# Attention outputs stored later, a third buffer for the final rows, and q and v laid out in pairs of blocks

## The chip, the cores and the metric

The kernel is one launch on one core of a Trainium2 chip. The metric is device time of the whole launch in microseconds, lower is better.

## The reference

Three stages follow one another on 2304 tokens (4 sequences of 576) of width 512, all in float32:

```
attn_out = windowed attention, 8 heads of 64 (4 with the last 32 tokens,
           4 with every 4th of the last 128), softmax, times v
x   = attn_out as (2304, 512)
e   = argmax(x @ w_gate)                      # one of 8 experts for each token
x   = softmax gate * sigmoid gate * (relu(x @ w1[e]) @ w2[e])    # 512 -> 1024 -> 512
out = relu(x @ w_in) ** 2 @ w_out             # 512 -> 2048 -> 512
```

## The kernel before

**Attention** (`attention`, L307) goes through 18 blocks of 128 tokens. Iteration i of its loop (L632, i = 0 to 14) does, in PE's order: `tr(i)` (L449, four transposes of block i's probabilities), the scores of block i + 2 (`qk`, L416), the transposes of block i - 1's output (`xt`, L503), and probabilities times v (`pv_mm`, L465). DVE, POOL and ACT make the softmax between them. Every few blocks a group of tokens is routed: router scores (`lg`, L518), ranks (`route4`, L569 to L572), and `scatter` (L611), an indirect DMA from POOL that writes each token's number into its expert's list in `meta_d`. Blocks 15 to 17 follow the loop in code written out by hand (from L676).

**Transfers** go nearly all through SP's queue, which issues in program order. Each DMA signals one of eight semaphores in turn, so it is issued only when the one eight places ahead of it has landed. The loads are q (`load_q`, L328), k (`load_k`, L335) and v with a column of ones (`load_v`, L346), usually two blocks at a time; v goes to every second partition, so a load of it is two DMAs. A buffer's next load waits until PE has read the last: q has three buffers of two blocks, `vb` holds four blocks, `kz` six. A **store** of a block pair (`store`, L491) writes the attention output `x` to `x_d` in HBM with three DMAs: 256 KB for the heads of the plain window (L495, 128 rows outermost), and for each block 128 KB for the dilated heads (L497), whose outermost dimension is 4, the rows inside it 32. Before, `x` has three buffers of two blocks, and the pair of blocks i - 2 and i - 1 is stored in iteration i = 2, 4, ..., 14.

**The way into the experts.** `choose` (L176) picks the fullest expert from the counts without the last three blocks. SP then reads its number and loads its first weights (`raw`, L117), its list (`mt`, L137) and more weights. POOL gathers 240 token rows from `x_d` (`gather(0)`, L143, two indirect DMAs), which may name any token of blocks 0 to 14 and so waits for all their stores. ACT and DVE split the weights (`conv_w`, L124 and L125) and the transposed tokens into two parts, and the first expert matmul starts (L792). From there PE runs nearly without a gap through the experts and the two passes of the last layer.

**The last layer's second pass** (`down2`, L898) adds, for each of six token blocks of 384, three final tiles of 128 rows: DVE adds the first pass's part into `os` (L919), and POOL scatters `os` to `out` (L920). `os` has two buffers (tag `ys`). `narrow` (L285) uses tag `fa`, also two buffers, only until the first pass ends.

Of the kernel before, what the change touches and what calls it, by code (L numbers as in the profile page):

```python
# [10 lines left out]
F32 = mybir.dt.float32  # L11
F32R = mybir.dt.float32r
# [10 lines left out]
B, H, S, D = 4, 8, 576, 64  # L23
P = 128
NT = B * S
NB = NT // P
# [4 lines left out]
COLS = [{1: 1, 2: 2}.get(len(r), 4) for r in GROUPS]  # L31
NG = len(GROUPS)
EARLY = GROUPS[NG - 1][0]
E = 8
DM = H * D
FF = 1024
# [9 lines left out]
NSPILL = 32  # L46
TB = 384
NTB = NT // TB

FA = 6  # L50

# [2 lines left out]
def attention_experts_kernel(ctx: ExitStack, tc: tile.TileContext, qB, kB, vB, wg, wE, wF, consts, rows, ids, out):  # L54
    nc = tc.nc
    cpool = ctx.enter_context(tc.tile_pool(name="cpool", bufs=1))
    dpool = ctx.enter_context(tc.tile_pool(name="dpool", bufs=1, space=DRAM))
    rp = ctx.enter_context(tc.tile_pool(name="rp", bufs=1))
# [25 lines left out]
    nspill = cpool.tile([1, 1], I32, name="nspill")  # L84
    mt = cpool.tile([P, E + 1, 3, 4], I32, name="mt")

    slots = [rp.tile([P, 2, 1024], F32R, name=f"slot{i}") for i in range(8)]
    free = list(range(8))

    def raw_tile():  # L90
        return stg.tile([P, 1024], F32, tag="raw", name="raw", bufs=3)
# [215 lines left out]
    def attention():  # L307
        st = ExitStack()
        c2 = st.enter_context(tc.tile_pool(name="c2", bufs=1))
# [4 lines left out]
        masks = c2.tile([P, 4, 2, 64], F32, name="masks")  # L314
        tri32 = c2.tile([P, P], F32, name="tri32")
        kz = c2.tile([P, 2, 4, (LAP + 1) * P], F32, name="kz")
        vb = c2.tile([P, 4, 2, 4, 4, D + 1], F32, name="vb")
        q_t = {}

        def warm(n):  # L320
# [4 lines left out]

        def load_q(i, n):
            q = wk.tile([P, 2, 4, P], F32, tag="q", name="q", bufs=3)
            nc.sync.dma_start(out=q[:, 0:n].rearrange("p i a s -> p i (a s)"), in_=qB[i:i + n].rearrange("i p s -> p i s"))  # L328
            for j in range(n):
                q_t[i + j] = q[:, j]  # L330

# [11 lines left out]
        def load_v(i, n, engine=nc.sync):  # L343
            j = i % 4
            for h2 in range(2):
                engine.dma_start(  # L346
                    out=vb[h2:P:2, j:j + n, h2].rearrange("p i a c e -> p i (a c e)"),
                    in_=vB[i:i + n, h2].rearrange("i m e -> m i e"),
                )

        def clear_k(t, first, second):
# [1 line left out]
            second.memset(kz[:, 1, :, P * t:P * t + P], 0.0)  # L353

        def clear_v(j, h2, engine):
            engine.memset(vb[:, j, h2], 0.0)

        load_q(0, 1)
        clear_k(1, nc.vector, nc.gpsimd)
# [94 lines left out]
        def pv_mm(i, apart=False):  # L454

            pt = pt_t.pop(i)
            if apart:
                o = [ps_s.tile([P, 2, 256], F32, tag="s", name="o2") for _ in range(2)]
            else:
                t = ps_1.tile([P, 4, 256], F32, tag="o", name="o")  # L460
                o = [t[:, 0:2], t[:, 2:4]]
            v = vb[:, i % 4]
            for p in range(4):
                for c in range(4):
                    nc.tensor.matmul(  # L465
                        out=o[p // 2][32 * c:32 * c + 32, p % 2, 0:130], lhsT=pt[:, p, 32 * c:32 * c + 32], rhs=v[:, :, p, c, :], start=True, stop=True
                    )
            o_t[i] = [t] if not apart else o

        def pv_x(i):  # L470
            for a, o in enumerate(o_t.pop(i)):
                n = o.shape[1]
                oh = o[:, :, 0:130].rearrange("p a (h e) -> p a h e", h=2)
                rs = wk.tile([P, 4, 2, 1], F32, tag="rs", name="rs")[:, 0:n]
                nc.vector.tensor_scalar(out=rs, in0=oh[:, :, :, 64:65], scalar1=1e-9, scalar2=None, op0=ALU.add)
                rr = wk.tile([P, 4, 2, 1], F32, tag="rr", name="rr")[:, 0:n]
                nc.vector.reciprocal(out=rr, in_=rs)
                if i % 2 == 0 and a == 0:
                    x_t["pair", i // 2] = wk.tile([P, 2, DM], F32, tag="x", name="x", bufs=3)
                x = x_t["pair", i // 2][:, i % 2]  # L480
                nc.vector.tensor_tensor(
                    out=x[:, 256 * a:256 * a + 128 * n].rearrange("p (a h d) -> p a h d", a=n, h=2), in0=oh[:, :, :, 0:64],
                    in1=rr.to_broadcast([P, n, 2, 64]), op=ALU.mult,
                )
            x_t[i] = x
# [5 lines left out]
        def store(i, m, engine=nc.sync):  # L491
            a = i % 2
            x = x_t["pair", i // 2]
            d = x_d[P * i:P * i + m * P]
            engine.dma_start(out=d[:, 0:256].rearrange("(n p) c -> p n c", n=m), in_=x[:, a:a + m, 0:256])  # L495
            for n in range(m):
                engine.dma_start(out=d[P * n:P * n + P, 256:512].rearrange("(j r) c -> r j c", r=4), in_=x[:, a + n, 256:512])  # L497
# [134 lines left out]
        for i in range(EARLY):  # L632
            tr(i)
            ex(i + 1)
            qk(i + 2)
            t = (i + 2) % LAP
            n = i + 2 - t + LAP
            if t == 2 and n < NB:
                load_k(n, 2)
            if t == 4 and n + 2 < NB:  # L640
                wrap()
                load_k(n + 2, min(3, NB - n - 2))
            if i > 0 and i % 2 == 0:
                store(i - 2, 2)
            if i % 2 == 0 and i + 6 < NB:
                load_q(i + 6, 2)
            if i == 0:
                load_consts()
            if i == 3:
                clear()  # L650
            if i == 3:
                nc.vector.tensor_copy(tri, tri32)
                nc.vector.tensor_copy(cs[:, 0, :], io8)
            for a, g in ((2, ends.get(i - 2)), (4, ends.get(i - 3))):
                if g is not None and g < NG - 3:
                    scatter(g, range(a - 2, min(a, COLS[g])))
            if i > 0:
                xt(i - 1)
            g = ends.get(i - 1)
            if g is not None:  # L660
                route4(g)
            pv(i)
            if i % 2 == 1 and i + 3 < NB:
                load_v(i + 3, 2)
            if i in ends:
                lg(ends[i])
                route1(ends[i])
                route2(ends[i])
                route3(ends[i])
            if g is not None:  # L670
                route5(g)
                route6(g)
                if g == NG - 3:
                    scatter(g)
# [68 lines left out]
    def experts():  # L743
# [2 lines left out]
        rp2 = st.enter_context(tc.tile_pool(name="rp2", bufs=1, reuse_waits="tile"))  # L746
        wp = st.enter_context(tc.tile_pool(name="wp", bufs=1, reuse_waits="tile"))
        ps = st.enter_context(tc.tile_pool(name="ps", bufs=1, space=PSUM, reuse_waits="tile"))
        for i in range(8, 16):
            slots.append(rp2.tile([P, 2, 1024], F32R, name=f"slot{i}"))  # L750
            free.append(i)

# [145 lines left out]
        def down2(b, f, js=range(TB // P)):  # L898
# [3 lines left out]
            for j in js:  # L902
# [4 lines left out]
                nc.tensor.matmul(out=o_t[j], lhsT=h[:, a], rhs=w[:, 1], start=False, stop=False)  # L907
                nc.tensor.matmul(out=o_t[j], lhsT=l[:, a], rhs=w[:, 0], start=False, stop=last)  # L908
                if last:
                    s = wp.tile([P, 512], F32, tag="ys", name="os", bufs=2)  # L910
                    t = b * (TB // P) + j
                    if f < FA:
                        if j % 2:
# [200 lines left out]
def _layout(inputs):  # L1114
# [17 lines left out]

    q, k, v = heads["q"], heads["k"], heads["v"]
    qb = np.concatenate([pairs(plain(q, 0, P), P), pairs(dilated(q, 0, 32).reshape(NB, H // 2, P, D), P)], axis=3)
    qB = np.ascontiguousarray(qb).reshape(NB, P, 4 * P)
    kp = k[:H // 2].reshape(2, 2, NT, D).transpose(1, 3, 0, 2)
    kd = dilated(k, 0, 32).reshape(NB, 2, 2, P, D).transpose(2, 4, 1, 0, 3).reshape(2, D, 2, NT)
    kB = np.ascontiguousarray(np.concatenate([kp, kd], axis=2))
# [1 line left out]
    vp = plain(one, -32, 160)  # L1140
    vp = np.stack([vp[:, :, 32 * c:32 * c + 64] for c in range(4)], axis=2)
    vb = np.concatenate([vp, dilated(one, -32, 64)], axis=1)
    vB = np.ascontiguousarray(vb.reshape(NB, 4, 2, 4, 64, D + 1).transpose(0, 2, 4, 1, 3, 5)).reshape(NB, 2, 64, 16 * (D + 1))
    g = np.zeros((DM, 32), f)
    g[:, 0:E] = inputs["moe_w_gate"]
    g[:, E:2 * E] = inputs["moe_w_output_gate"]
# [48 lines left out]
```

## Time and profile before

| what | us |
|---|---|
| three runs | 778.11, 779.4, 782.96 |
| median | 779.4 |
| the profiled execution | 777.51 |
| its span (first to last instruction) | 775.8 |
| attention's loop, from its first `tr` to the one after it | 13.0 to 82.6 |
| first expert matmul | 113.6 |
| PE's last matmul | 762.9 |

In the rows below, a timeline row gives start and duration in us, engine, line, operation, tiles, shapes and count, and in brackets the idle time before it with what ended it. SPq rows are DMAs being issued, not moved. A window row gives the stretch, its length, then busy us (and instructions) of PE, PEld (weight loads), DVE, ACT and POOL, the clock granted to PE as a share, the mean busy share of the 16 DMA engines, and GB/s. A row of waits gives who waited for whom, us in total, times, and the longest.

### The profile page before, as it was taken

What the parts mean: (1) busy time and instruction counts of PE and PEld (TensorE: products, weight loads), DVE (VectorE), ACT (ScalarE), POOL (GpSimd) and SP (SyncE); (2) the same over time, 40 slices, a digit from 0 to 9 for tenths busy, and PEclk for the clock granted to TensorE, in tenths of its full rate; (3) what the DMA queues carried; (4) which work ended last, traced back from release to release, by engine and by line L of the source; (5) the groups of instructions that cost most, each with busy time, mean ns of one, the idle gap of its engine ahead of it and who ended that gap; (6) DMA issues with size and microseconds to landing.
All of it is one profiled execution on the core that took longest, in us unless ns stands there. A gap on an engine that the chain in (4) does not pass through costs nothing. (4 is left out here: it accounts for less than half of the span.)

```text
span 775.8 us, 13876 instructions
## 1 busy us (share of the span) xinstructions
PE 725.0 (93%) x5371; PEld 658.2 (85%) x5371; DVE 435.3 (56%) x888; ACT 327.2 (42%) x647; POOL 95.5 (12%) x104
## 2 busy tenths in 40 slices
PE   7877659999999999999999999999999999999993
PEld 4655539999999999999989998999899998888892
DVE  6756747776657666867686768732424233333321
ACT  2533425554455565655555555632223223223220
POOL 5233535011011010000000000000101010000101
PEclk9999979999999999999999999999999999999997
DMA  8999567575565676775344443230303020120201
GB/s 273 289 284 263 141 195 217 171 248 189 162 223 177 210 240 202 208 229 149 116 125 146 154 135 117 74 123 1 122 1 123 1 95 28 47 77 0 83 1 44
DMA packets 55057, 110.15 MB, mean 142 GB/s; under 512 B 9513, under 2 KB 30890, under 8 KB 54986
## 3 DMA queue, kind: packets, MB, share of 16 engines
q1 hardware_dynamic: 45338, 93.35, 39.2%
q0 software_dynamic: 4176, 10.57, 3.9%
q10 hardware_dynamic: 5472, 5.29, 2.0%
q8 instruction: 44, 0.72, 0.4%
q14 instruction: 27, 0.22, 0.1%
HBM read 89.42 MB, written 19.80 MB: 141 GB/s over the span
## 5 line engine op out<-in xcount | busy, mean ns | idle before, releaser
L792 PE MATMUL hp<-xh,slot 128*128 128x384 f32 (+6 forms) x672 | 214.2, 319 | 2.9 <-DVE hl L807 1.6
L794 PE MATMUL hp<-xh,slot 128*128 128x384 f32 (+6 forms) x672 | 213.9, 318 | 0.0
L793 PE MATMUL hp<-xl,slot 128*128 128x384 f32 (+6 forms) x672 | 213.3, 317 | 0.0
L792 PEld LDWEIGHTS hp<-xh,slot 128*128 128x128 f32 x672 | 126.6, 188 | 6.9 <-DVE hl L807 2.0
L793 PEld LDWEIGHTS hp<-xl,slot 128*128 128x128 f32 x672 | 126.5, 188 | 3.0
L794 PEld LDWEIGHTS hp<-xh,slot 128*128 128x128 f32 x672 | 126.4, 188 | 0.0
L879 DVE SCALAR_TENSOR_TENSOR g<-hp,r 128x384 f32<-128x384 f32 x96 | 53.3, 555 | 119.9 <-ACT r L878 119.4
L906 PE MATMUL op<-slot,gh 128*128 128x512 f32 x288 | 112.5, 391 | 2.3 <-ACT gh L881 2.3
L908 PE MATMUL op<-slot,gl 128*128 128x512 f32 x288 | 114.0, 396 | 0.0
L907 PE MATMUL op<-slot,gh 128*128 128x512 f32 x288 | 113.4, 394 | 0.0
L125 DVE TENSOR_TENSOR slot<-raw,slot 128x1024 fp32r<-128x1024 f32 x64 | 77.8, 1225 | 52.5 <-ACT slot L124 52.2
L878 ACT ACTIVATE r<-hp 128x384 f32<-128x384 f32 x96 | 46.9, 489 | 141.8 <-PE hp L794 141.1
L793 PE MATMUL yp<-hl,slot 128*128 128x240 f32 (+6 forms) x288 | 85.1, 295 | 2.3 <-DVE hl L807 2.3
L792 PE MATMUL yp<-hh,slot 128*128 128x240 f32 (+6 forms) x288 | 86.1, 299 | 0.1
L794 PE MATMUL yp<-hh,slot 128*128 128x240 f32 (+6 forms) x288 | 84.7, 294 | 0.0
L883 DVE TENSOR_TENSOR gl<-g,gh 128x384 fp32r<-128x384 f32 x96 | 53.5, 558 | 44.0 <-ACT gh L881 43.5
L881 ACT CAST gh<-g 128x384 fp32r<-128x384 f32 x96 | 49.2, 513 | 63.3 <-DVE g L879 62.9
L920 POOL DMA_INDIRECT out<-os,idc x18 | 17.6, 977 | 467.9 <-DVE os L919 466.4
L124 ACT CAST slot<-raw 128x1024 fp32r<-128x1024 f32 x64 | 66.4, 1050 | 16.3 <-DMA raw<-in_wE 12.1
L906 PEld LDWEIGHTS op<-slot,gh 128*128 128x128 f32 x288 | 54.2, 188 | 12.6 <-ACT gh L881 3.5
L908 PEld LDWEIGHTS op<-slot,gl 128*128 128x128 f32 x288 | 54.0, 188 | 12.5 <-DVE gl L883 1.2
L907 PEld LDWEIGHTS op<-slot,gh 128*128 128x128 f32 x288 | 54.0, 188 | 9.6
(152 smaller groups left out, 875.0 us busy)
## 6 DMA issues: line engine op xcount, KB each, us to landing
raw<-in_wE SPq DMA_DIRECT2D x63, 512.0 KB
raw<-in_wF SPq DMA_DIRECT2D x32, 512.0 KB
yr<-yT_d SPq DMA_DIRECT2D x48, 192.0 KB
vb<-in_vB SPq DMA_DIRECT2D x16, 520.0 KB
part_d<-os SPq DMA_DIRECT2D x18, 256.0 KB
raw<-part_d SPq DMA_DIRECT2D x18, 256.0 KB
q<-in_qB SPq DMA_DIRECT2D x8, 512.0 KB
x_d<-x SPq DMA_DIRECT2D x22, 128.0 KB
```

The lines of the kernel that those rows point to most:

```text
L124: nc.scalar.copy(out=hi, in_=raw)
L125: nc.vector.tensor_tensor(out=lo, in0=raw, in1=hi.bitcast(F32), op=ALU.subtract)
L792: nc.tensor.matmul(out=out, lhsT=wh, rhs=mh, start=first, stop=False)
L793: nc.tensor.matmul(out=out, lhsT=wh, rhs=ml, start=False, stop=False)
L794: nc.tensor.matmul(out=out, lhsT=wl, rhs=mh, start=False, stop=last)
L878: nc.scalar.activation(out=r, in_=p[:, :TB], func=ACTF.Relu)
L879: nc.vector.scalar_tensor_tensor(out=q, in0=p[:, :TB], scalar=0.0, in1=r, op0=ALU.max, op1=ALU.mult)
L881: nc.scalar.copy(out=h, in_=q)
L883: nc.vector.tensor_tensor(out=l, in0=q, in1=h.bitcast(F32), op=ALU.subtract)
L906: nc.tensor.matmul(out=o_t[j], lhsT=h[:, a], rhs=w[:, 0], start=first, stop=False)
L907: nc.tensor.matmul(out=o_t[j], lhsT=h[:, a], rhs=w[:, 1], start=False, stop=False)
L908: nc.tensor.matmul(out=o_t[j], lhsT=l[:, a], rhs=w[:, 0], start=False, stop=last)
```

## The change

The stores of blocks 0 to 13 move from iterations 2 to 14 to iterations 9 to 14, by a table; `x` gets nine buffers of two blocks instead of three, and the room comes from weight slots: only three of the sixteen exist during attention, the rest are made after it. q and v are laid out in HBM (and v on the chip) so that two blocks of one partition stand in one run of bytes: a pair of q is 128 rows of 4 KB instead of 256 of 2 KB, a half of a pair of v 64 rows of 8320 bytes instead of 128 of 4160. The third final tile of each token block takes tag `fa` in place of `ys`.

```diff
+STORES = {9: (0,), 10: (2,), 11: (4,), 12: (6,), 13: (8, 10), 14: (12,)}
+VN = 16 * (D + 1)
+VL = -(-2 * VN // 128) * 128
...
-    slots = [rp.tile([P, 2, 1024], F32R, name=f"slot{i}") for i in range(8)]
-    free = list(range(8))
+    slots = [rp.tile([P, 2, 1024], F32R, name=f"slot{i}") for i in range(3)]
+    free = list(range(3))
...
-        vb = c2.tile([P, 4, 2, 4, 4, D + 1], F32, name="vb")
+        vb = c2.tile([P, 2, 4, 4, 4, D + 1], F32, name="vb")
...
-            nc.sync.dma_start(out=q[:, 0:n].rearrange("p i a s -> p i (a s)"), in_=qB[i:i + n].rearrange("i p s -> p i s"))
+            a = i % 2
+            nc.sync.dma_start(out=q[:, 0:n].rearrange("p i a s -> p (i a s)"), in_=qB[i // 2, :, a:a + n].rearrange("p i s -> p (i s)"))
...
-                    out=vb[h2:P:2, j:j + n, h2].rearrange("p i a c e -> p i (a c e)"),
-                    in_=vB[i:i + n, h2].rearrange("i m e -> m i e"),
+                    out=vb[h2:P:2, h2, j:j + n].rearrange("p i a c e -> p (i a c e)"),
+                    in_=vB[i // 2, h2, :, VN * (i % 2):VN * (i % 2 + n)],
...
-                    x_t["pair", i // 2] = wk.tile([P, 2, DM], F32, tag="x", name="x", bufs=3)
+                    x_t["pair", i // 2] = wk.tile([P, 2, DM], F32, tag="x", name="x", bufs=NB // 2)
...
-            if i > 0 and i % 2 == 0:
-                store(i - 2, 2)
+            for a in STORES.get(i, ()):
+                store(a, 2)
...
-        for i in range(8, 16):
+        for i in range(3, 16):
             slots.append(rp2.tile([P, 2, 1024], F32R, name=f"slot{i}"))
...
-                    s = wp.tile([P, 512], F32, tag="ys", name="os", bufs=2)
+                    s = wp.tile([P, 512], F32, tag="fa" if j == 2 and f >= FA else "ys", name="os", bufs=2)
```

`clear_v`, `pv_mm` and the host's layout of q and v follow the new order of dimensions.

SP's queue before, from the load of v for blocks 6 and 7 on (`vb` is v, `kz` k, `x_d<-x` a store, `zm` the zeros of the lists):

```order
L346 DMA vb<-in_vB 64x2x1040 x2
L495 DMA x_d<-x 128x2x256
L497 DMA x_d<-x 4x32x256 x2
L328 DMA q<-in_qB 128x2x512
L335 DMA kz<-in_kB 64x4x256 x2
L346 DMA vb<-in_vB 64x2x1040 x2
L495 DMA x_d<-x 128x2x256
L497 DMA x_d<-x 4x32x256 x2
L328 DMA q<-in_qB 128x2x512
L335 DMA kz<-in_kB 64x4x384 x2
```

The same place after the change (line numbers are those of the changed kernel):

```order
L352 DMA vb<-in_vB 64x2080 x2
L334 DMA q<-in_qB 128x1024
L341 DMA kz<-in_kB 64x4x256 x2
L352 DMA vb<-in_vB 64x2080 x2
L334 DMA q<-in_qB 128x1024
L341 DMA kz<-in_kB 64x4x384 x2
```

Each round of loads loses the store that stood in it, and q and v have half as many, longer rows.

SP's queue before, from the last load of k to the first weights:

```order
L335 DMA kz<-in_kB 64x4x128 x2
L495 DMA x_d<-x 128x2x256
L497 DMA x_d<-x 4x32x256 x2
L346 DMA vb<-in_vB 64x2x1040 x2
L495 DMA x_d<-x 128x2x256
L497 DMA x_d<-x 4x32x256 x2
L495 DMA x_d<-x 128x256
L497 DMA x_d<-x 4x32x256
L94 TENSOR_LOAD e_t
L117 ISA
L117 DMA raw<-in_wE 128x1024
```

The same place after:

```order
L341 DMA kz<-in_kB 64x4x128 x2
L501 DMA x_d<-x 128x2x256
L503 DMA x_d<-x 4x32x256 x2
L501 DMA x_d<-x 128x2x256
L503 DMA x_d<-x 4x32x256 x2
L501 DMA x_d<-x 128x2x256
L503 DMA x_d<-x 4x32x256 x2
L352 DMA vb<-in_vB 64x2080 x2
L501 DMA x_d<-x 128x2x256
L503 DMA x_d<-x 4x32x256 x2
L501 DMA x_d<-x 128x256
L503 DMA x_d<-x 4x32x256
```

Three stored pairs now stand between the last k and the last v, where one stood, and three more pairs stand ahead of that k; the reading of the expert's number and its weights still come behind the store of block 14. The order of instructions on PE, DVE, ACT and POOL is the same in both kernels.

## Rows read from the trace of the kernel before

**Rows 1.** Windows: the loop's first iterations, then the rest of it

```profile
13.00:26.00 13.00, 13.00 (x264) 10.23 (x268) 8.53 (x17) 6.88 (x15) 4.81 (x8) 0.87 0.96 322
26.00:86.00 60.00, 44.94 (x1014) 35.16 (x1006) 38.55 (x135) 24.12 (x62) 24.07 (x24) 0.97 0.91 274
```

**Rows 2.** Timeline: `tr` of iterations 0, 2 and 3, and of block 15

```profile
13.00 0.80 PE L449 MATMUL pt<-ident,pr 128*128 128x128 f32 x4 [2.33 <-DMA ident<-in_consts]
...
20.28 0.66 PE L449 MATMUL pt<-ident,pr 128*128 128x128 f32 x4
...
23.49 0.66 PE L449 MATMUL pt<-ident,pr 128*128 128x128 f32 x4
...
82.61 0.66 PE L449 MATMUL pt<-ident,pr 128*128 128x128 f32 x4
```

**Rows 3.** Waits of PE from 13 to 87 us, those that DMAs ended

```profile
PE o L465 <- DMA vb<-in_vB: 5.6, 3, 2.0
PE s L416 <- DMA kz<-in_kB: 2.6, 3, 1.5
...
PE s L416 <- DMA q<-in_qB: 2.2, 2, 1.5
```

**Rows 4.** DMA view of 10 to 22 us, loads alone; GB/s in 40 slices

```profile
GB/s 372 395 391 406 359 287 353 410 383 369 373 407 413 442 395 405 363 408 376 396 404 385 325 353 360 395 374 291 378 367 356 375 347 383 363 379 375 410 379 372
DMA packets 2538, 4.52 MB, mean 377 GB/s; under 512 B 215, under 2 KB 1423, under 8 KB 2537
```

**Rows 5.** DMA view of 30 to 86 us: total, and the stores issued

```profile
DMA packets 9836, 15.21 MB, mean 272 GB/s; under 512 B 978, under 2 KB 7017, under 8 KB 9825
...
x_d<-x SPq DMA_DIRECT2D x14, 128.0 KB
x_d<-x SPq DMA_DIRECT2D x6, 256.0 KB
```

**Rows 6.** Windows at the end of the loop's transfers

```profile
88.00:90.00 2.00, 1.31 (x37) 0.94 (x35) 1.97 (x8) 0.96 (x3) 1.79 (x2) 1.00 0.31 87
90.00:92.00 2.00, 1.07 (x8) 0.83 (x8) 1.82 (x11) 1.07 (x2) 0.99 (x1) 1.00 0.23 75
92.00:93.00 1.00, 1.00 (x35) 0.82 (x33) 0.86 (x8) 0.65 (x2) 0.92 (x1) 1.00 0.07 12
```

**Rows 7.** Timeline from the last store of the loop to the first expert matmul

```profile
85.02 0.50 SPq L497 DMA_DIRECT2D x_d<-x  x1
...
88.80 1.09 PE L465 MATMUL o<-vb,pts 128*32 128x130 f32 x32 [0.58 <-ACT pts L451]
...
93.37 0.38 SPq L117 DMA_DIRECT2D raw<-in_wE  x1
...
95.95 0.39 SPq L137 DMA_DIRECT2D mt<-meta_d  x1
...
100.10 1.04 ACT L124 CAST slot<-raw 128x1024 fp32r<-128x1024 f32 x1 [3.21 <-DMA raw<-in_wE]
...
101.95 1.37 POOL L143 DMA_INDIRECT xg<-x_d,mt  x1 [8.90 <-DMA x_d<-x]
...
113.61 0.38 PE L792 MATMUL hp<-xh,slot 128*128 128x240 f32 x1 [1.35 <-DVE xl L159]
```

**Rows 8.** Waits from 395 to 776 us, the two around `os`

```profile
DVE os L919 <- DMA out<-os,idc: 25.8, 6, 5.4
...
PE op L906 <- ACT gh L881: 2.3, 3, 0.9
```

**Rows 9.** Timeline: one of PE's three gaps in the second pass

```profile
684.50 0.50 PE L906 MATMUL op<-slot,gh 128*128 128x512 f32 x1 [0.94 <-ACT gh L881]
```

**Rows 10.** Timeline of the last three tiles

```profile
762.46 0.39 PE L908 MATMUL op<-slot,gl 128*128 128x512 f32 x1
762.50 0.97 POOL L920 DMA_INDIRECT out<-os,idc  x1 [0.39 <-DVE os L919]
764.03 0.69 DVE L919 TENSOR_TENSOR os<-op,raw 128x512 f32<-128x512 f32 x1 [1.81 <-DMA out<-os,idc]
765.00 0.97 POOL L920 DMA_INDIRECT out<-os,idc  x1 [1.53 <-DVE os L919]
```

More of the change, by code (lines that the diff above doesn't have):

```diff
@@ L355, in clear_v @@
         def clear_v(j, h2, engine):
-            engine.memset(vb[:, j, h2], 0.0)
+            engine.memset(vb[:, h2, j], 0.0)
         load_q(0, 1)
@@ L461, in pv_mm @@
                 o = [t[:, 0:2], t[:, 2:4]]
-            v = vb[:, i % 4]
+            v = vb[:, :, i % 4]
             for p in range(4):
@@ L1134, in _layout @@
     qb = np.concatenate([pairs(plain(q, 0, P), P), pairs(dilated(q, 0, 32).reshape(NB, H // 2, P, D), P)], axis=3)
-    qB = np.ascontiguousarray(qb).reshape(NB, P, 4 * P)
+    qB = np.ascontiguousarray(qb.reshape(NB // 2, 2, P, 4 * P).transpose(0, 2, 1, 3))
     kp = k[:H // 2].reshape(2, 2, NT, D).transpose(1, 3, 0, 2)
@@ L1142, in _layout @@
     vb = np.concatenate([vp, dilated(one, -32, 64)], axis=1)
-    vB = np.ascontiguousarray(vb.reshape(NB, 4, 2, 4, 64, D + 1).transpose(0, 2, 4, 1, 3, 5)).reshape(NB, 2, 64, 16 * (D + 1))
+    vB = np.zeros((NB // 2, 2, 64, VL), f)
+    vB[..., :2 * VN] = vb.reshape(NB // 2, 2, 4, 2, 4, 64, D + 1).transpose(0, 3, 5, 1, 2, 4, 6).reshape(NB // 2, 2, 64, 2 * VN)
     g = np.zeros((DM, 32), f)
```

## Prediction

> **What bounds the kernel now.** I read the windows first, then the waits, the DMA view and the timeline at the place where attention hands over to the experts, and last the waits of the second pass of the last layer.
>
> The windows split the loop in two [rows 1]. From 13 to 26 us PE is busy throughout and 322 GB/s arrive. From 26 to 86 us PE is busy 44.94 of 60 us, so it idles 15.1 us, while the DMA engines are busy 91% of the time; yet they move less, 274 GB/s. The timeline gives the pace: iteration 2, still without a wait, lasts 23.49 - 20.28 = 3.21 us, and the 13 iterations up to `tr` of block 15 last 62.3 us, or 4.79 each [rows 2]. Of the idle 15.1 us the waits put 5.6 + 2.6 + 2.2 = 10.4 us down to loads of v, k and q [rows 3]. So the loop is bound by its transfers, and could end 10.4 to 15.1 us earlier.
>
> Why do the busy engines move less? With loads alone they move 377 GB/s [rows 4]. From 30 to 86 us they move 15.21 MB at 272 GB/s [rows 5]; at 377 that would take 40.3 us instead of 56, so 15.7 us are lost. The stores there are 14 x 131 KB + 6 x 262 KB = 3.41 MB, 9.0 us at 377. By this a stored pair (6.5 of them in that stretch) costs (15.7 + 9.0) / 6.5 = 3.8 us of all engines, instead of 1.4. The windows at the end, when nearly only stores are left, show what a store is: 31% and then 23% of the engines busy, 4 or 5 of 16, at 87 and 75 GB/s [rows 6]. The dilated half, with an outermost dimension of 4, uses about four engines; a load issued behind it is complete only when its share on those four is through.
>
> The way into the experts is the second bound [rows 7]. The last store of the loop is issued at 85.02, and the windows show engines at work until about 92.5 [rows 6]. The first weights are issued at 93.37, and ACT gets them at 100.10 after a wait of 3.21; the list is issued at 95.95, and the gather starts at 101.95 after 8.90 us of idle POOL. The view names the store for that wait, but stores have long been done by 92.5: what came last can only be the list. The first expert matmul comes at 113.61, 11.66 us behind the gather, and from there PE hardly stops. A microsecond at the gather is a microsecond of the kernel.
>
> **The change part by part.**
>
> *Stores out of the loop's first half.* Nothing is computed differently, and PE, DVE, ACT and POOL keep their order; SP's queue loses one stored pair (3 DMAs) from each round of loads up to iteration 8, and gets three more pairs between the last k and the last v. Until iteration 9 the loads should run as in [rows 4], and the loop's waits of [rows 3] go: I take the loop to end about 10 us earlier, at 72 to 73.
>
> That is no gain yet, since the gather needs every store of blocks 0 to 14. What those stores ask of the four engines is the same bytes, in the same pieces, and so the same work. In the loop of before these four were the busy ones nearly throughout (loads lasted as long as they did), and nothing in the change takes work from them. They have the same total to do from 13 us on, so I take the last store to land where it did, at about 92.5, though PE is done far earlier. What does move is the issue of weights and list. Before, they were issued at 93.37 and 95.95, when nearly nothing was left to move; now the fullest expert is known about 10 us earlier, and both stand in the queue behind the last stores (at most eight DMAs are under way, so they are issued when the train has about eight left). They land when their bytes have followed the stores: two blocks of 524 KB of weights, 2 x 1.4 us at 377 GB/s, make 92.5 + 2.8 = 95.3. The gather starts at 95.3 instead of 101.95: **-6.6 us**. Ends for this term: 0, if the list still takes 6 us behind the last store, and -15.1, the whole idle time of the loop, if the four engines had time to spare.
>
> The Trainium skill ("DMA: Bandwidth & Descriptors", section "Why a DMA increments its semaphore by 16 and not by 1") says that a DMA is spread over the largest number of engines up to 16 that divides the slowest dimension of both its sides, and on the lowest-numbered ones. For the dilated store that is 4, and always the same 4; the 23% busy share [rows 6] agrees. It speaks against this change: putting such stores later makes none of them wider, and a train of them queues on the four engines. If the engines were instead shared evenly, the sum would be that of the second rival below.
>
> *v of blocks 16 and 17* stands behind six pairs. By the same reckoning (the four engines' work ahead of it is unchanged) it lands about where it did, and `pv_mm(16)`, at 88.80 before [rows 7], stays near there while PE waits some 10 us in front of it. Behind it on PE are only blocks 16 and 17 and their routing, which the gather does not need. Cost 0; the third rival is the price if this is wrong.
>
> *Paired rows.* q and v go in rows of twice the length: in the stretch of [rows 5], 7017 of 9836 packets are under 2 KB, and it is not shown what longer ones cost. The slices of loads alone reach from 287 to 442 GB/s [rows 4]; on the 14.3 MB of q and v of the whole attention, against 377, that is from 11.9 us longer to 5.5 us shorter. But these are the loads, which PE no longer waits for in either case if the stores are gone from beside them: I take 0, the mean of the row, and keep the ends for the range.
>
> *Nine x buffers and fewer weight slots.* DVE's writes of `x` wait for no store any more, and the three slots that exist are all that the attention stage fills; the others are made after it, where a first write may wait for a late store of the same room. DVE's writing of `x` was not among the waits that mattered: 0.
>
> *The third final buffer.* In the second pass DVE waits 25.8 us in six places for a scatter to leave `os`; PE feels it only in three gaps of 2.3 us together, the longest 0.9 [rows 8], one of them at 684.50 [rows 9]. With the third buffer DVE writes all three tiles of a token block at once: **-2.3 us** (from 0, if ACT's `gh` is late for a reason of its own, to -2.3). At the very end DVE waits 1.81 us and starts the last tile at 764.03, 1.2 us behind PE's last matmul, which starts at 762.46 and takes 0.39; it would then start at 762.95 and end at 763.64. POOL's scatter before it ends at 763.47, so the last one starts at about 763.64 + 0.28 (its distance from DVE's end before) = 763.9 instead of 765.00 [rows 10]: **-1.1 us**. In all -3.4 us. The use of tag `fa` ends with the first pass, so it takes no buffer from anybody.
>
> *Sum.* -6.6 - 2.3 - 1.1 = -10.0 us. The profiled execution took 777.51 (span 775.8 and 1.7 around it), which becomes 767.5. The median of the three runs stands 1.9 above the profiled one; I carry that over: 779.4 - 10.0 = **769.4 us**.
>
> **The rivals.**
>
> *Everything that the loop gains reaches the gather.* For it: the waits [rows 3] are loads, and 272 against 377 GB/s [rows 4, 5] may be a matter of switching between reads and writes, which a train of writes alone avoids. Against it: the train alone runs at 75 to 87 GB/s [rows 6]. The gain at the head is then 10.4 to 15.1, say 12.8, and with the tail 16.2: 763.2 us.
>
> *The head gains nothing.* The four engines get further behind than I think, or the list stays 6 us behind the last store as it was (93.37 and 95.95 may not be set by the loop at all). For it: 6 us from issue to use with little traffic, after 92 us only 12 GB/s [rows 6, 7]. Only the tail's 3.4 us are left: 776.0 us.
>
> *Slower: v of blocks 16 and 17 waits behind the train.* Iteration 9 begins between 20.28 + 7 x 3.21 = 42.8 and 20.28 + 7 x 4.79 = 53.8, say at 48. From there to that load stand six pairs and the loads of about two pairs of blocks (q 0.52, k 0.52, v 1.07 MB each pair, 4.2 MB, 11 us at 377). If a pair costs not 3.8 us but all its 524 KB at 75 GB/s, 7.0 us [rows 6], v lands at 48 + 6 x 7.0 + 11 = 101, and `pv_mm(16)` starts 12.2 us late. ACT's wait of 3.21 us for weights [rows 7] is the slack I can see; 9.0 us remain and reach the first expert matmul, less 3.4 of the tail: 785.0 us. It decides from about 6 us for a pair: then v lands at 95, and 3 us of loss cancel the tail's gain. Against it: 3.8 us is what pairs cost in the loop, and the load of v overlaps the train on the other twelve engines.
>
> **How the numbers follow.** About 1% (7.8 us: 771.6 and 787.2) is what a measurement of this kernel can tell from no change. Forecast 0.50, full gain 0.18, only the tail 0.22, slower by v 0.10. The forecast's own range is 765 to 775, so some 0.7 of it counts as faster; with the full gain that is 0.35 + 0.18, and 0.53 in all. Same: 0.15 of the forecast, 0.22 of the tail alone and a little of the v case, 0.39. Slower by more than 1% needs v later than about 103, by longer packets' bad end [rows 4] or a dearer pair: 0.08. The range reaches from just below the full gain, 761, to 782, between the tail alone and the v case.
>
> **What would show it.** Right: no waits of PE for v, k or q in the loop and `tr` of block 15 near 72; stores issued from iteration 9 on and a stretch of 10 us or more with about a quarter of the engines busy; a long wait of PE at `pv_mm(16)`, and the last store near 92; weights and list issued well before 93, the gather near 95, the first expert matmul near 107; in the second pass no wait of DVE for `out`, and the last scatter about 1.1 us closer to PE's last matmul. Wrong: a gather at or behind 101.95 (head gains nothing), or near 88 (the four engines were not full); a first expert matmul that waits for `pv_mm(16)`; waits for loads that remain in iterations 3 to 8, where no store runs, which would mean that the loads themselves are the limit.

## The result, and the profile after

The changed kernel takes 773.72 us (median of 6) beside 781.57 for the kernel before: a ratio of 0.9892, 95% interval 0.9861 to 0.9922, or 8.4 us less (the two medians are 7.9 apart). Measured once more beside other kernels (experiment e9) it took 775.0 beside 779.0: 0.9949, interval 0.9926 to 0.9971, 4.0 us less. The two intervals just miss each other: the gain is clear of noise, but its size is known only as 4.0 in one measurement and 8.4 in the other (2.3 to 10.9 by their intervals). The forecast was 10.0 less, with a range of 761 to 782.

The profiled execution took 771.45 us, its span is 769.8. First the windows, which answer to [rows 1]:

```profile
13.00:26.00 13.00, 12.74 (x301) 10.03 (x302) 9.63 (x19) 7.21 (x16) 5.52 (x9) 1.00 0.92 325
26.00:86.00 60.00, 49.41 (x1032) 36.00 (x1024) 39.62 (x141) 23.66 (x61) 25.64 (x26) 0.98 0.85 259
```

PE is busy 49.41 of 60 us instead of 44.94, so the loop did become freer. The timeline has the transposes of block 15 at 76.47 instead of 82.61 [rows 2]:

```profile
76.47 0.66 PE L455 MATMUL pt<-ident,pr 128*128 128x128 f32 x4
```

The waits of PE from 13 to 87 us (compare [rows 3]) show what went and what came:

```profile
PE o L471 <- issue: 4.2, 9, 1.0
PE s L422 <- DMA kz<-in_kB: 1.5, 1, 1.5
PE lg L524 <- issue: 1.4, 4, 0.4
PE pt L455 <- issue: 1.2, 1, 1.2
...
PE o L471 <- DMA vb<-in_vB: 0.3, 1, 0.3
```

Waits for loads fell from 10.4 to 1.8 us. But 6.8 us now end on "issue", which is idle time for which the profile shows no cause; before it was 2.8. Both are one execution: in e9 the same program has 5.8 for loads and 5.0 on "issue". The last part of the way to the experts answers to [rows 6, 7], first as windows, then as a timeline:

```profile
84.00:86.00 2.00, 1.65 (x15) 1.24 (x15) 1.34 (x7) 0.21 (x1) 0.00 (x0) 0.50 0.87 144
86.00:88.00 2.00, 0.60 (x7) 0.45 (x5) 1.97 (x10) 1.10 (x3) 1.04 (x1) 0.50 0.84 294
88.00:90.00 2.00, 0.00 (x0) 0.00 (x0) 1.82 (x10) 0.24 (x1) 1.17 (x2) 0.50 0.42 152
90.00:92.00 2.00, 0.14 (x4) 0.17 (x8) 0.31 (x3) 0.00 (x0) 0.80 (x1) 0.50 0.37 121
```

```profile
89.83 0.97 POOL L617 DMA_INDIRECT meta_d<-idsb,di  x1 [0.30 <-issue]
91.12 0.54 SPq L122 DMA_DIRECT2D raw<-in_wE  x1
91.86 1.96 PE L471 MATMUL o<-vb,pts 128*32 128x130 f32 x32 [5.26 <-DMA vb<-in_vB]
95.97 0.39 SPq L142 DMA_DIRECT2D mt<-meta_d  x1
100.37 1.05 POOL L148 DMA_INDIRECT xg<-x_d,mt  x1 [9.57 <-DMA x_d<-x]
112.16 0.38 PE L799 MATMUL hp<-xh,slot 128*128 128x240 f32 x1 [1.35 <-DVE xl L164]
```

The list is issued at 95.97, where it was issued before at 95.95. The gather starts only 1.58 us earlier and the first expert matmul 1.45 us. PE waits 5.26 us for v of blocks 16 and 17, and its granted clock is half from 84 to beyond 92.

At the other end the waits of DVE for `out` [rows 8] and PE's gaps [rows 9] are gone, and the last tiles (compare [rows 10]) follow one another:

```profile
757.03 0.69 DVE L927 TENSOR_TENSOR os<-op,raw 128x512 f32<-128x512 f32 x1 [0.67 <-PE op L915]
757.99 0.97 POOL L928 DMA_INDIRECT out<-os,idc  x1 [0.38 <-DVE os L927]
```

So of the profiled execution's 6.06 us, 1.45 were gained at the head and the rest behind it. And 1.45 is not more than two executions of the same attention code differ by: in e3, whose attention is that of the kernel before, the first expert matmul comes at 115.37 instead of 113.61, and in e9, the changed kernel again, at 114.37, which is later than before.

### The profile page after: what moved, and what is told of

The parts are those of the page before. It is cut to its first block, busy times and chain, and to the rows that moved or that the text cites. A ratio compares the mean times of both kernels' runs of the same rounds, so it can differ in the third digit from the quotient of the medians.

```text
span 769.8 us, 13866 instructions
## 1 busy us (share of the span) xinstructions
PE 726.6 (94%) x5371; PEld 659.5 (86%) x5371; DVE 437.4 (57%) x888; ACT 327.6 (43%) x647; POOL 95.3 (12%) x104
## 4 chain that ended last, share of the span: by engine, by line
PE 81%; DMA 6%; DVE 5%; issue 2%; ACT 2%; another core or an unknown queue 1%; SPq 1%; ACTq 0%; POOL 0%; POOLq 0%; DVEq 0%
PE hp L799 12%; PE hp L801 12%; PE hp L800 12%; PE op L914 9%; PE op L915 9%; PE op L913 9%; PE yp L800 4%; PE yp L799 4%; PE yp L801 4%; PE o L471 1%; PE xp L172 1%; PE s L422 1%; DVE slot L130 1%; DMA q<-in_qB 1%; DMA raw<-in_wE 1%
## 5 line engine op out<-in xcount | busy, mean ns | idle before, releaser
L913 PE MATMUL op<-slot,gh 128*128 128x512 f32 x288 | 112.0, 389 | 0.0
L130 DVE TENSOR_TENSOR slot<-raw,slot 128x1024 fp32r<-128x1024 f32 x64 | 77.8, 1225 | 47.9 <-ACT slot L129 47.2
L129 ACT CAST slot<-raw 128x1024 fp32r<-128x1024 f32 x64 | 66.4, 1051 | 12.5 <-DMA raw<-in_wE 8.8
L915 PEld LDWEIGHTS op<-slot,gl 128*128 128x128 f32 x288 | 54.0, 188 | 11.4
```

The costliest lines, as they stand in the source:

```text
L129: nc.scalar.copy(out=hi, in_=raw)
L130: nc.vector.tensor_tensor(out=lo, in0=raw, in1=hi.bitcast(F32), op=ALU.subtract)
L913: nc.tensor.matmul(out=o_t[j], lhsT=h[:, a], rhs=w[:, 0], start=first, stop=False)
```

## The experiments

Each ratio is to the kernel before, run beside the experiment.

**e1 and e2: the dilated stores made wider.** Four DMAs a pair, 32 rows outermost, instead of two with 4:

```diff
-            for n in range(m):
-                engine.dma_start(out=d[P * n:P * n + P, 256:512].rearrange("(j r) c -> r j c", r=4), in_=x[:, a + n, 256:512])
+            for r in range(4):
+                engine.dma_start(out=d[:, 256:512].rearrange("(n j r) c -> r j n c", n=m, r=4)[r], in_=x[32 * r:32 * r + 32, a:a + m, 256:512])
```

> The changed kernel, with the dilated half of each stored pair written by four DMAs of 32 rows outermost (64 KB each, one per residue of the token number by 4) in place of two with 4 outermost; same bytes, same places in the queue. If the four engines are what the train of stores costs (theory A), the stretch of a quarter-busy engines at 80 to 98 us goes: v of blocks 16 and 17 lands before 86 (91.7 now), the last store before 92 (97.8 now), PE's wait of 5.3 us for v and most of its 4.2 us without instructions go, the first expert matmul comes at 104 to 108 instead of 112.2, and the kernel takes 765 to 770 us. If the head is held by something else, the list's scatter and load or the pace of PE alone (theory B), the first expert matmul stays within 1.5 us of 112.2 and the time at 772 to 775.

> The kernel before, with only that same edit of the dilated stores: they stay in iterations 2 to 14. Theory A: the 15.7 us that stores cost the loop beyond their bytes go, PE's waits for v, k and q in the loop fall from 10.4 to under 3 us, the block 15 transposes start near 73 to 76 instead of 82.6, the first expert matmul at 104 to 107 instead of 113.6, and the kernel takes 771 to 774 us against 781.6. Theory B: waits as before, first expert matmul within 1.5 us of 113.6, time within 0.5% of before.

Measured: e1 772.22, ratio 0.9878 (0.984 to 0.9916), the changed kernel's own; first expert matmul at 113.65, and PE waits for v 10.8 us in all. e2 779.98, ratio 0.9993 (0.9974 to 1.0012): no change. Windows of e2 at the end of the loop's transfers, to be held against [rows 6]:

```profile
84.00:86.00 2.00, 1.41 (x44) 0.86 (x42) 1.38 (x8) 1.68 (x5) 1.39 (x3) 1.00 0.35 100
86.00:88.00 2.00, 1.09 (x11) 0.47 (x11) 0.00 (x0) 0.00 (x0) 1.70 (x2) 1.00 0.20 44
88.00:90.00 2.00, 1.01 (x14) 0.74 (x12) 0.72 (x4) 0.13 (x1) 0.23 (x1) 0.72 0.04 4
90.00:92.00 2.00, 1.36 (x14) 1.12 (x16) 1.93 (x9) 0.78 (x3) 0.79 (x1) 0.50 0.00 0
```

The stores were through by 90, some 2.5 us sooner than before, though SP was done issuing them at 86.3 instead of 85.5. The Trainium skill's rule on the number of engines ("DMA: Bandwidth & Descriptors", section "Why a DMA increments its semaphore by 16 and not by 1") agrees with that, but no gain follows from it. With the transfers at 0 to 4 GB/s from 88 to 92, the gather of e2 still came later than before:

```profile
93.23 0.99 POOL L613 DMA_INDIRECT meta_d<-idsb,di  x1 [0.98 <-DVE rs L475]
94.52 0.97 POOL L613 DMA_INDIRECT meta_d<-idsb,di  x1 [0.30 <-issue]
104.03 1.05 POOL L143 DMA_INDIRECT xg<-x_d,mt  x1 [8.53 <-DMA x_d<-x]
```

From the last scatter of blocks 13 and 14 to the gather it is 9.5 us with idle transfers; it was 9.9 in the kernel before and 10.5 after the change. In e5 and e11 below, which have no stores in the loop, it is 9.5 and 10.6. That is a chain of latencies (scatter, list, gather), and no train of stores is needed for it. In its form of four engines, theory A falls.

**e3: the third final buffer alone.**

```diff
-                    s = wp.tile([P, 512], F32, tag="ys", name="os", bufs=2)
+                    s = wp.tile([P, 512], F32, tag="fa" if j == 2 and f >= FA else "ys", name="os", bufs=2)
```

> The kernel before, with only the third final buffer (every third final tile of the second pass under the other tag). By the prediction: DVE's waits for out go, PE's three gaps of 2.3 us in the second pass go, and the last scatter starts 1.1 us closer to PE's last matmul: 3.4 us less, ratio near 0.9956. Rival: the gaps go, but the end of the program stays 13 us behind PE's last matmul as it did in the changed kernel, so only 2.3 us: ratio near 0.997.

Measured: 776.34, ratio 0.9943 (0.9922 to 0.9965): 4.4 us less, 2.7 to 6.1. The buffer alone gives half of the gain first measured, and all of the second. In the profiled execution the span shrank by 0.1 us only, because its head came 1.76 us later and its expert stage began at half clock (last section); what PE gained behind that is given below.

**e4 and e8: other iterations for the stores.** In the changed kernel:

```diff
-STORES = {9: (0,), 10: (2,), 11: (4,), 12: (6,), 13: (8, 10), 14: (12,)}
+STORES = {2: (0,), 4: (2,), 6: (4,), 8: (6,), 10: (8,), 12: (10,), 14: (12,)}
```

and in e8 `{6: (0,), 7: (2,), 8: (4,), 9: (6,), 10: (8,), 12: (10,), 14: (12,)}`.

> The changed kernel, with the pairs stored in iterations 2 to 14 again as before; the paired rows, the nine x buffers and the third final buffer stay. If moving the stores is worth the 1.5 us by which the first expert matmul came earlier, it comes at 113 to 114 and the kernel takes 1 to 3 us more than the changed one (774 to 777). If paired rows were what sped up the loop (iteration 3 to 8 at 346 GB/s), it stays at 112 or earlier and the time is that of the changed kernel. If moving the stores was worth the 6.6 us predicted and something else took it back, 117 to 119 and 778 to 781.

> The changed kernel with the pairs stored in iterations 6, 7, 8, 9, 10, 12 and 14 instead of 9 to 14 (between it and the kernel with stores in 2 to 14, which took 775.8). If what deferral gains is the free early loop, half of its 2 to 3 us goes: 774 to 775. If what it costs is the train ahead of v of blocks 16 and 17 and of the list (theory A), v lands before 88, the last scatter of blocks 13 and 14 lands 2 us earlier and the time falls to 770 to 772.

Measured: e4 775.82, ratio 0.993 (0.9903 to 0.9957); e8 772.72, ratio 0.9954 (0.9925 to 0.9983; before stood at 776.58 beside it). The profiled execution of e4 was the slowest of its six (778.14), with the first expert matmul at 118.76: that alone would fit the third branch of the expectation, while the median fits the first. In e8 PE waits only 0.34 us in front of the product of block 16, and not for v; the first expert matmul is at 111.95. Storing early, the other edits kept, gives in e4 a ratio between the changed kernel's two. By these ratios moving the stores is worth from -1.5 to 2.9 us, and this series can't tell that from nothing. The other edits without it give 5.5 us (e4), 1.1 more than the buffer alone: paired rows and nine `x` buffers can't be told from nothing.

**e5 and e11: no stores of pairs in the loop** (only that of block 14 remains), and gathers that read rows of q. In the changed kernel (in the kernel before, the call of `store` goes):

```diff
-STORES = {9: (0,), 10: (2,), 11: (4,), 12: (6,), 13: (8, 10), 14: (12,)}
+STORES = {}
...
-                out=t[:n], out_offset=None, in_=x_d[0:known],
+                out=t[:n], out_offset=None, in_=qB.rearrange("a p b s -> (a p b) s")[0:known],
```

> The changed kernel without any store of blocks 0 to 14's pairs in the loop (only block 14's and the last three remain), and with every gather of token rows reading q's rows, which have the same size, in place of the stored x. Left out: the stores of the pairs, and the right values in the experts' input; PE, DVE, ACT and POOL do the same work. If the train of stores is still what holds the head (theory A, now for all 16 engines), the first expert matmul comes at 103 to 107 and the kernel takes 765 to 768 us. If the head is held by PE's own pace at the end of the loop and by the chain scatter, list, gather (theory B), it comes within 2 us of the changed kernel's, 110 to 114, and the time is 771 to 774.

> The kernel before without the stores of the pairs in the loop, its gathers reading q's rows instead of the stored x; scatters in place. Left out: these stores and the right values in the experts' input. Theory A, the prediction's 3.8 us a pair: the loop ends 10 to 15 us earlier and the kernel takes 11 to 15 us less than before (0.981 to 0.986). Theory C: what is saved is about what the changed kernel without stores saved beyond its third buffer, 4 to 6 us (0.992 to 0.995), with holes in the loads after pairs of scatters that remain.

Measured: e5 766.91, ratio 0.9874 (0.9846 to 0.9903), first expert matmul at 106.15; e11 772.14, ratio 0.9906 (0.9872 to 0.994). e5 meets theory A's numbers as they were put, in microseconds; but before stood at 776.58 beside it, 5 us under its first median, and by the ratios e5 is only 1.4 to 5.8 us under the changed kernel (0.9892 and 0.9949, of 781.6 and 776.6). So the train of stores still costs that kernel something. In single executions that is 6 us at the first expert matmul and 4.3 us of span, since e5's expert stage began at half clock. In e5 PE no longer waits for v of blocks 16 and 17, and the gather starts at 94.27. e11 lies between the two theories' numbers. Its window and its main waits:

```profile
26.00:86.00 60.00, 49.15 (x1079) 38.03 (x1073) 42.68 (x152) 25.23 (x64) 27.49 (x28) 0.94 0.77 222
```

```profile
PE o L465 <- issue: 4.0, 2, 3.5
PE pt L449 <- issue: 1.5, 1, 1.5
PE o L465 <- DMA vb<-in_vB: 1.5, 2, 1.0
...
PE s L416 <- issue: 1.1, 1, 1.1
PE s L416 <- DMA kz<-in_kB: 1.0, 1, 1.0
```

Without these stores PE still idles 10.85 of 60 us, and the transposes of block 15 start at 77.53. So all the stores of the loop cost 82.6 - 77.5 = 5.1 us of its length in these two executions, and 15.1 - 10.9 = 4.2 us of PE's idle time in a window that holds more work in e11. The changed kernel, at 76.5 in one execution and 79.12 in the other (e9), has already got most of that.

**e6 and e10: no scatters of the lists of blocks 0 to 12.** These are 14, not 12 as the first expectation says. In both kernels:

```diff
-                if g is not None and g < NG - 3:
-                    scatter(g, range(a - 2, min(a, COLS[g])))
+                pass
...
-                if g == NG - 3:
-                    scatter(g)
```

> The changed kernel without POOL's scatters of the token lists of blocks 0 to 12 (12 of the scatters before the experts; those of blocks 13 and 14 and of the last group stay). Left out: these entries of the lists; the lists are read and the rows gathered in the same number. Theory C: the scatters stall the DMA queues, and with them PE's supply of instructions, which is where the changed kernel lost 4 us between the transposes of blocks 15 and 16 (idle that ended on nothing the profile shows, while four scatters ran in a row). It expects those 8.9 us to fall to 4 to 5, no idle of that kind over 1 us there, loads in the loop closer to 377 GB/s (40 to 50 us: 300 or more against 221), the first expert matmul at 103 to 107, and 764 to 768 us. If the scatters are innocent (theory B), the gap stays and the time is 771 to 774.

> The kernel before without the scatters of the lists of blocks 0 to 12, stores in place. Left out: these entries of the lists; everything else runs in the same number. Theory C (the scatters stall the loads, not the stores): the stretch from 30 to 86 us moves its bytes at 310 GB/s or more instead of 272, PE's waits for v, k and q in the loop fall from 10.4 to under 5 us, the transposes of block 15 start near 74 instead of 82.6, and the kernel takes 8 to 12 us less than before (ratio 0.985 to 0.990). Theory A (the stores, as the prediction had it): 2 us less at most.

Measured: e6 762.38, ratio 0.981 (0.9781 to 0.9839); e10 769.94, ratio 0.9873 (0.9829 to 0.9917). Some 2 us of both stand at the very end, where with shorter lists the span stops 11 us behind PE's last matmul instead of 13, so the head is read from the first expert matmul: 105.58 against 112.16 (e6), 110.86 against 113.61 (e10). In both, other stretches moved too: e6 lost 4.1 us again from the first expert matmul to the first `op` matmul, part of it at half clock, and in e10 PE's gaps in the second pass went although the third buffer is not there, 2.7 us; why is not shown. So of the 7.0 us that e10's span is shorter, only 2.75 stand at the head. The slices of the DMA view show what the scatters do. From 38 to 50 us, first e5 (scatters, no stores), then e6 (no scatters; its stores start behind this):

```profile
DMA  8999898999975479999137598933701289999999
GB/s 356 436 412 416 361 388 319 374 401 398 397 290 221 139 172 107 113 123 41 31 128 113 51 37 36 47 26 21 31 20 36 103 216 307 389 441 451 496 437 431
DMA packets 1072, 2.79 MB, mean 233 GB/s; under 512 B 217, under 2 KB 773, under 8 KB 901
```

```profile
DMA  9999999998598999779989999994896799996989
GB/s 389 390 412 466 324 359 360 305 361 361 250 387 373 427 384 383 311 280 309 268 297 360 381 374 424 369 213 162 268 313 250 305 416 388 388 291 248 372 316 342
DMA packets 1456, 4.07 MB, mean 339 GB/s; under 512 B 143, under 2 KB 1012, under 8 KB 1199
```

and the second pair of scatters of that group in e5 (the first pair starts at 36.04 and 37.42):

```profile
39.60 0.93 POOL L617 DMA_INDIRECT meta_d<-idsb,di  x1 [0.17 <-issue]
40.83 0.92 POOL L617 DMA_INDIRECT meta_d<-idsb,di  x1 [0.30 <-issue]
```

Each slice is 0.3 us. From 41.9 us, behind these two scatters, the loads run at 20 to 172 GB/s for over 5 us, much of it with the engines shown as busy, and no store is in the loop. It is not that nothing was there to load: SP issued k, v and q between 40.87 and 45.01 us and nothing more before 50, and the rate is back at 307 to 496 GB/s from 47.9 on. Without scatters the same 12 us have 339 GB/s on average. But behind the first pair nothing of the kind is seen (290 GB/s or more up to 41.6), so not every pair makes a hole, and what decides it is not shown. Nor are the holes a large part of what [rows 5] shows below 377 GB/s: without scatters (e10) the stretch from 26 to 86 us moved 283 GB/s against 274, PE waited 6.5 us for loads instead of 10.4 (under 5 expected), and block 15 started at 80.14, 2.5 us earlier (74 expected). Theory C is right in kind for that much. In e6 the 8.9 us from block 15 to block 16 fell to 4.2 as expected, but that shows nothing: e8, with all its scatters, has 4.2 too (80.68 to 84.91), e9, the changed kernel again, 5.7, and e3 9.3 where the same code before had 4.8. PE's waits for loads rose to 11 us in e6, 8.1 of them one wait for v of blocks 16 and 17.

**e7 and e12: scatters placed otherwise**, nothing left out. e7 moves those of blocks 11 and 12 behind the loop; e12 issues the four of each of the first three groups in a row (its edit):

```diff
-            for a, g in ((2, ends.get(i - 2)), (4, ends.get(i - 3))):
-                if g is not None and g < NG - 3:
-                    scatter(g, range(a - 2, min(a, COLS[g])))
+            g = ends.get(i - 2)
+            if g is not None and g < NG - 3:
+                scatter(g)
```

> The changed kernel with the two scatters of blocks 11 and 12 moved on POOL from the end of iteration 14 to right ahead of those of blocks 13 and 14. Nothing is left out. Theory C: only two scatters instead of four run beside the product of block 15, so the idle there halves, the transposes of block 16 come some 2 us earlier; the last scatter stands behind two more (up to 2.6 us), so the gather gains nothing or loses 1 us: 772 to 775 us. Theory B: block 16 as now, and the last scatter 1 to 2.6 us later: 774 to 776.

> The changed kernel with the four scatters of each of the first three groups issued in a row, two iterations after the group's last block, in place of two and two. Nothing left out. If the loads are stalled once for each burst of scatters (theory C1), three stalls fewer of about 2 us each: 768 to 771 us, 3 to 5 us under the changed kernel beside it. If each scatter stalls them by itself (theory C2): within 2 us of the changed kernel; POOL holds back a softmax by 2.6 us three times, so rather slower than faster.

Measured: e7 773.4, ratio 0.9953 (0.9932 to 0.9974); block 16 came 4.2 us after block 15, but PE then waited 7.9 us for v of blocks 16 and 17, and the gather came only at 99.91. e12 773.78, ratio 0.9929 (0.9904 to 0.9955), beside e9 with 775.0: within 2 us, as C2 had it, and C1's 3 to 5 us did not come. Placing scatters otherwise doesn't buy back what leaving them out shows.

**e9: the changed kernel again.**

> The changed kernel once more, unchanged, beside the next three on one chip, so that they can be compared with it there. 0.989 of the kernel before by its first measurement; between 0.986 and 0.992.

Measured: 775.0, ratio 0.9949 (0.9926 to 0.9971), outside what was expected. In its profiled execution PE waits 8.4 us for v of blocks 16 and 17 (5.3 in the first), and the first expert matmul is at 114.37. No experiment gave a kernel that clearly beats the changed one.

## Why the prediction was right and wrong

**The sign was right, and the size by the first measurement; most of the reason was not.** It put 6.6 us at the head and 3.4 at the tail. Measured are 4.4 for the third buffer (e3), and from nothing to 4 for all the rest. That the sum still came out within the range is luck: the tail was put too small and the head too large, which partly cancel, and the second measurement, 4.0 us, lies near the rival with the tail alone (3.4).

**The third buffer: mechanism right, its parts mis-sized.** From the first `op` matmul to the start of PE's last, it takes 762.46 - 364.82 = 397.64 us before and 397.85 in e2 (two buffers), but 393.83 in e3, after the change (756.60 - 362.77) and in e9 (three buffers). That is 3.8 us on PE, where the forecast had 2.3: the row of waits [rows 8] gives only the idle time, and PE lost more around each gap. At the gap of [rows 9] the matmul behind the gap, at 684.50, started 1.29 us after the one ahead of it:

```profile
683.21 0.34 PE L794 MATMUL hp<-xh,slot 128*128 128x384 f32 x1
...
684.83 0.40 PE L907 MATMUL op<-slot,gh 128*128 128x512 f32 x1
```

and after the change 679.63 - 679.45 = 0.18 us later:

```profile
679.45 0.33 PE L801 MATMUL hp<-xh,slot 128*128 128x384 f32 x1
679.63 0.39 PE L913 MATMUL op<-slot,gh 128*128 128x512 f32 x1
679.86 0.40 PE L914 MATMUL op<-slot,gh 128*128 128x512 f32 x1
```

So 1.1 us for an idle time of 0.94, and the next starts are 0.33 apart instead of 0.23. The 1.1 us at the very end did not come: the last scatter moved up as forecast, 1.39 us behind the start of PE's last matmul instead of 2.54, but the span still ends 13.2 us behind that (769.8 - 756.60), as it did before (775.8 - 762.46 = 13.3). So 3.9 us of e3's 4.4 are seen in the traces. What the end waits for is not shown.

**"By this a stored pair costs 3.8 us": this step failed.** It charged to the stores all that the loop moved below 377 GB/s. That rate was read between 10 and 22 us [rows 4], a stretch without stores, but also without scatters. e11 took all stores out: block 15 came 5.1 us earlier, 0.8 us for each of the 6.5 pairs. e10 took the scatters out: 2.5 us earlier. What is left of the 10 us has no owner in these runs. Hence "the loop to end about 10 us earlier" became 6.1, and 3.5 in e9. (e11's whole saving is 7.3 us, with 4.7 and 10 as its ends, where 3.8 us a pair would have given 11 to 15.)

**"I take the last store to land where it did, at about 92.5": failed.** From 84 us on only stored rows of `x` travel in packets of 1024 bytes; the last of them that belongs to the loop starts at 92.24 before, but at 97.36 after the change and at 97.93 in e9. With wide stores (e1, e2) the kernel's time did not change, so their width is not what counts. The Trainium skill's rule (the section cited above) agrees with the traces, but the result that hung on it does not hold.

**"v of blocks 16 and 17 ... Cost 0": failed in its reason.** The product of block 16 came 3.1 us later than before (91.86 against 88.80), and 5.2 later in e9. The prediction saw only that the gather does not need these blocks. But the first expert matmul does, through the order of work on ACT and DVE: ACT copies the last blocks' transposes before it splits the first weights (L129), and DVE does the last routing (up to L735) before it scales the gathered rows (L158). Before, both came early and waited for DMAs: ACT 3.21 us for the weights [rows 7], and DVE for the gathered rows:

```profile
106.58 0.15 DVE L728 COPY cs<-rk 1x8 f32<-1x8 f32 x1
107.67 0.55 DVE L153 TENSOR_SCALAR xg<-xg,mt 128x512 f32<-128x512 f32 x1 [0.94 <-DMA xg<-x_d,mt]
```

After the change neither waits for a DMA:

```profile
100.19 1.06 ACT L129 CAST slot<-raw 128x1024 fp32r<-128x1024 f32 x1
106.71 0.15 DVE L735 COPY cs<-rk 1x8 f32<-1x8 f32 x1
106.79 1.07 DVE L158 TENSOR_SCALAR xg<-xg,mt 128x512 f32<-128x512 f32 x2
```

and e9 has the same order 2 us later:

```profile
94.00 1.96 PE L471 MATMUL o<-vb,pts 128*32 128x130 f32 x32 [8.42 <-DMA vb<-in_vB]
108.79 0.87 DVE L158 TENSOR_SCALAR xg<-xg,mt 128x512 f32<-128x512 f32 x2
114.37 0.38 PE L799 MATMUL hp<-xh,slot 128*128 128x240 f32 x1 [1.35 <-DVE xl L164]
```

In the six traces in which PE waits over 4 us for this v (after, e1, e6, e7, e9, e12) the first expert matmul follows the start of that product after 19.7 to 20.5 us; in the other eight after 22.2 to 26.4. So late stores delay this load, and the load sets the way into the experts: the mechanism of the third rival, and its sign, "a first expert matmul that waits for `pv_mm(16)`". Its size is small: with the 11.66 us that lay between gather and first expert matmul before, the matmul would stand at 112.0 instead of 112.16, and in e9 at 112.4 instead of 114.37. So it cost some 0 to 2 us, an estimate from these rows; no run moved this load alone ahead of the stores.

**"The list lands when its bytes have followed the stores": failed.** Its issue stayed at 95.97, because it reads what the last scatter of blocks 13 and 14 writes. Two steps of the chain of waits after the change, with start, length and what it was:

```profile
89.83 6.12 DMA meta_d<-idsb,di
...
95.97 0.39 SPq L142
```

That scatter starts 2.3 us sooner than before (92.08), but takes 6.1 us to land instead of 3.9, beside the late stores and loads; the list then takes 4.4 us to the gather instead of 6.0. And 4 of the 6.1 us that block 15 had gained were gone by block 16 (85.40 after, 87.41 before), in PE's "issue" idle. From the start of that scatter to the gather it takes 10.5 us after the change, and 11.4 in e9, against 8.8 to 9.9 in the kernels with the stores in their old places (before, e2, e3, e4); but e11, without stores, has 10.6, so the late stores are not shown to be the cause. The rival "the head gains nothing" gave 776.0; with the buffer's true 4.4 it gives 777.2 against 781.6 or 774.6 against 779.0. e9 measured that (775.0); the first measurement, 773.72, lies between it and the forecast.

**Right:** waits for loads nearly gone in the first profile (5.8 us of them are left in e9); no wait of DVE for `out`; paired rows and more `x` buffers within what can't be told from nothing.

**Open:** whether moving the stores gives nothing or 3 to 4 us (the changed kernel's two measurements differ by that), and what PE's "issue" idle is. It was 2.6 us in e6 and 6.8 in the changed kernel, yet 4.0 in e10 and 2.8 before, and 6.2 in e5 at other places; neither scatters nor stores alone explain it. At 80.9 us, in the longest such stretch of the changed kernel, one 16 KB packet of the instruction queue took 2.15 us, where most of them take 0.9 to 1.3; whether PE waited for it is not shown.

## What to carry to other kernels

A rate lost between two stretches is the price of a suspect only if nothing else differs between them; look for a stretch that lacks the suspect alone, or take the suspect out. An engine's idle time in a bound loop is often shared by several causes, and what one gives up another takes (10.4 us of load waits became 1.8, while idle time without a shown cause went from 2.8 to 6.8). Before a stage is shortened, follow the chain that leaves it: here scatter, list and gather cost 9.5 us even with idle transfers. And a delay is free only if no engine on the path stands behind it in program order: the gather did not need blocks 16 and 17, but ACT and DVE worked on them before they turned to the gathered rows.

## What the runs showed of the hardware

A pair of indirect DMAs that write 16 bytes for each of 128 tokens was followed by a hole of some 5 us in the loads of another queue, 20 to 172 GB/s with loads issued and no store in the loop, where the kernel without these scatters had 339 on average; the pair ahead of it was not (e5, e6). And the same code can meet either level of PE's clock: from 112 to 120 us the granted clock was 0.50 in e3 (half of full speed, 1.2 GHz) and 0.98 in the kernel before, and the first expert matmul took 0.57 us instead of 0.38. From there to the first `op` matmul e3 took 253.27 us, before 251.21.
